# One pool of eight PSUM banks for attention, handed out by a run of the instruction list while building, with a new table of nominal times

## The chip, the cores and the metric

The kernel runs on one core of a Trainium2 chip. The metric is the device time of one execution in microseconds (us), taken as the median of several runs. The core's engines, as the profile names them, are PE (TensorE: matrix products, and PEld, its weight loads), ACT (ScalarE), DVE (VectorE), POOL (GpSimd) and SP (SyncE, which issues most transfers). Products land in PSUM, which has eight banks that hold 512 float32 numbers per partition each; ACT and DVE carry results from there to SBUF.

## What is computed

An attention over 2 batches of 8 heads, whose queries are first averaged in pairs along the sequence, then two feed-forward blocks. All inputs and the output are float32.

```python
# attention: q, k, v of (2, 8, 1152, 64)
q_pool = q.reshape(B, H, S // 2, 2, D).mean(axis=3)
scores = scale * np.matmul(q_pool, k.transpose(0, 1, 3, 2))
scores = scores - np.max(scores, axis=-1, keepdims=True)
attn = np.exp(scores)
attn = attn / (np.sum(attn, axis=-1, keepdims=True) + 1e-09)
x = np.matmul(attn, v)                      # -> (1152, 512) tokens
# first block, 512 -> 2048 -> 512
h = x @ w_in
g = (a[0] + a[1]*h + a[2]*h**2 + a[3]*h**3) / (1 + abs(b[0])*abs(h) + abs(b[1])*h**2 + 1e-6)
x = g @ w_out
# second block, 512 -> 2048 -> 512
h = x @ w_in2
out = (np.maximum(h, 0) + np.log1p(np.exp(-np.abs(h)))) @ w_out2
```

## The kernel before

Each float32 operand of a product is split into a high and a low part (names in `h` and `l`: `ph` and `pl`, `xh` and `xl`, `gh` and `gl`), and a product is made of two or three products of the parts.

**Attention** works on eight pairs of heads, j = 0 to 7. A pair has 1152 query rows in nine tiles of 128, numbered 9j to 9j+8, and each row tile has 1152 keys in three pieces of 384. For each row tile t and piece e there is:

- `score` (kind S, line 459): PE multiplies queries and keys into a tile `s` in PSUM
- `rmax` (M and B, lines 466 and 470): DVE takes the negated maximum `nm` of each piece, then `mb` of the three
- `expo` (E, line 479): ACT makes `p`, the exponentials, and their sums
- `spread` (T, line 430): PE transposes `p` in three pieces into a tile `t` in PSUM. In mode A, two tiles of three, ACT casts `t` to `ph` (V, line 425) and DVE subtracts for `pl` (L, line 313). In mode B, one of three, ACT copies `t` to `c` in SBUF (line 529), and POOL makes `ph` (H, line 539) and `pl` (L, line 313) of it
- `pv` (P, line 559): for four groups of row tiles per pair, PE sums 18 value products each into a tile `pv` in PSUM
- `norm` and `xev`: POOL and DVE make the reciprocals `rc` of the sums; PE transposes them (R, line 430) into PSUM; ACT copies one half of `pv` to `u` (U, line 589), DVE adds the other half (U1, line 592) and multiplies by the reciprocals into `xs` (U2, line 601); POOL splits `xs` into `xh` and `xl`.

During a pair the next one is prepared: transfers `kq`, sums `pq`, transpositions `kt` and `qt`, their splits, and transfers that lay the parts where the scores want them (`dk`, `dq`, `dd`). In the last pair thirteen blocks of weights are loaded and split for the feed-forward blocks (names `wraw`, `pk`, `w`; kinds wl, w0 to w4).

**Order.** Nothing is issued where it is written. `op` records each step with a nominal time `when`: its row tile's number plus an offset of its kind from the tables `O`, `OT` (by row tile) and `OJ` (first and last pair). `run` sorts each engine's steps by `when`; that is the order on the engine. Steps are then emitted, of those at the heads of the engines' lists whose needs are met the one with the lowest `when`.

**Banks.** PSUM is divided by purpose: `pS` has four banks for `s`, `pT` three for `t` (transpositions of probabilities, reciprocals, keys and queries alike), `pA` one for `pv`. Within each the tiles take turns in the order of `when` of their first step: the m-th `s` waits until all steps on the (m-4)-th `s` are done (`need[u[0]].update(tiles[m - n])`).

**After attention** the three pools are released and two pools for the first feed-forward block are made: `ph_`, two buffers of two banks each, in which PE multiplies tokens and weights into `h` (line 970), and `pa_`, four banks for the second product (line 1019). Each `h` is two blocks of 12 matmuls. ACT works on it at lines 986 to 988 (`act1_a`), DVE at 993 to 995 (`act1_y`), then both finish the activation. These steps are ordered by the framework's own scheduler, which may put them between attention's last ones. The second feed-forward block follows (lines 1051 and 1073).

## Time and profile before

| | us |
|---|---|
| median of 3 runs | 725.07 (724.95 to 726.0) |
| the profiled execution | 724.6 |
| its span, first to last instruction | 722.7 |
| attention, up to the last value product | 310.0 |
| from there to the end | 412.7 |

The profile has one execution. A page gives each engine's busy time and its course over 40 slices; other views give single instructions in order of time, what an engine waited for, and the chain of work that ended last. The rows that matter stand further down. A wait's releaser is the instruction whose end let the waiting one go, as far as the semaphores tell; `PEld s L459 <- ACT p L479` reads: the weight load of a score waited for an exponential.

### The profile page before, as it was taken

The page shows a single profiled execution, that of the slowest core. Times are in us where ns is not written, and L with a number is a line of the kernel's source. Part 1 is how long each engine was busy: PE and PEld are TensorE (multiplying, and loading weights), DVE is VectorE, ACT ScalarE, POOL GpSimd, SP SyncE. Part 2 cuts the span into 40 slices and gives each one's busy share as a digit, 9 for nine tenths or more (in the row PEclk, how much of TensorE's full clock was granted, in tenths as well). Part 3 has the DMA queues.
Part 4 walks back from the last instruction along what each step waited for, and adds up shares of the span by engine and source line. Part 5 has one row for each costly group of instructions (what it writes and reads, how often), then busy time and mean ns, then how long its engine had stood idle before and what let it go on. Part 6 is the DMA issues. An engine that isn't in the chain of part 4 may idle for free.

```text
span 722.7 us, 11854 instructions
## 1 busy us (share of the span) xinstructions
PE 685.3 (95%) x4076; PEld 629.0 (87%) x4076; DVE 559.4 (77%) x1080; ACT 495.2 (69%) x1135; POOL 205.2 (28%) x357
## 2 busy tenths in 40 slices
PE   7898999999999987879999999999999999999997
PEld 6788888888889876679999999999899998998996
DVE  4787889898988899989999999999776675612122
ACT  3788889999988889966777777776554464423221
POOL 3667686868685744630000000000000000000000
PEclk8999999999999999999999999999999999999999
DMA  3364647372727353431111112211034333201011
GB/s 98 100 132 115 151 116 158 95 185 62 165 54 165 91 159 130 148 115 59 59 58 59 59 59 88 88 29 59 2 117 126 107 117 99 77 1 45 0 44 44
DMA packets 60395, 65.68 MB, mean 91 GB/s; under 512 B 21552, under 2 KB 49456, under 8 KB 60336
## 3 DMA queue, kind: packets, MB, share of 16 engines
q1 hardware_dynamic: 59152, 63.95, 32.8%
q10 hardware_dynamic: 1184, 0.98, 0.4%
q8 instruction: 32, 0.52, 0.3%
q14 instruction: 27, 0.22, 0.1%
HBM read 47.71 MB, written 2.36 MB: 69 GB/s over the span
## 4 chain that ended last, share of the span: by engine, by line
PE 60%; DVE 19%; ACT 12%; issue 4%; DMA 2%; SPq 1%; POOL 0%; DVEq 0%; ACTq 0%
PE acc L1073 14%; PE h L1051 13%; PE s L459 8%; PE t L430 8%; PE pv L559 7%; PE acc L1019 5%; PE h L970 4%; ACT p L479 4%; DVE nm L466 2%; ACT ph L425 2%; DMA wraw<-in_moe_w_in_dram 2%; DVE m L995 2%; DVE p L993 2%; DVE m L1005 2%; DVE pl L313 2%
## 5 line engine op out<-in xcount | busy, mean ns | idle before, releaser
L466 DVE TENSOR_REDUCE nm<-s 128x1 f32<-128x384 f32 x216 | 116.5, 550 | 23.4 <-PE s L459 22.1
L479 ACT ACTIVATE p<-s,mb 128x384 f32<-128x384 f32 x216 | 125.9, 593 | 5.1 <-DVE mb L470 4.6
L313 DVE TENSOR_TENSOR gl<-p,gh 128x384 fp32r<-128x384 f32 (+1 forms) x72 | 49.6, 689 | 91.5 <-ACT gh L1060 89.7
L430 PE MATMUL t<-ident,p 128*128 128x128 f32 x648 | 99.0, 276 | 8.8 <-ACT p L479 4.2
L970 PE MATMUL h<-xh,w 128*128 128x384 f32 x384 | 98.5, 335 | 3.5 <-DVE p L994 3.5
L1051 PE MATMUL h<-xh,w 128*128 128x384 f32 x384 | 98.4, 336 | 0.0
L1059 ACT ACTIVATE p<-h 128x384 f32<-128x384 f32 x48 | 23.6, 492 | 108.5 <-PE h L1051 108.5
L1019 PE MATMUL acc<-gh,w 128*128 128x384 f32 x384 | 93.1, 337 | 2.1 <-ACT gh L980 2.1
L430 PEld LDWEIGHTS t<-ident,p 128*128 128x128 f32 x648 | 79.0, 142 | 18.2 <-ACT p L479 9.6
L559 PE MATMUL pv<-ph,v 128*128 128x256 f32 (+1 forms) x288 | 89.5, 321 | 1.2 <-DVE u L592 0.6
L1073 PE MATMUL acc<-w,gh 128*128 128x512 f32 x288 | 89.5, 392 | 0.0
L313 DVE TENSOR_TENSOR pl<-t,ph 128x384 fp32r<-128x384 f32 (+1 forms) x160 | 80.3, 509 | 7.0 <-ACT ph L425 5.4
L425 ACT CAST ph<-t 128x384 fp32r<-128x384 f32 (+1 forms) x160 | 70.0, 453 | 18.8 <-PE t L430 12.7
L559 PE MATMUL pv<-pl,v 128*64 128x256 f32 (+1 forms) x288 | 77.4, 295 | 1.6 <-POOL pl L313 1.6
L313 POOL TENSOR_TENSOR pl<-c,ph 128x384 fp32r<-128x384 f32 (+1 forms) x80 | 75.0, 941 | 4.6
L1051 PEld LDWEIGHTS h<-xh,w 128*128 128x128 f32 x384 | 70.5, 188 | 4.3 <-ACT p L1059 0.4
L970 PEld LDWEIGHTS h<-xh,w 128*128 128x128 f32 x384 | 69.1, 188 | 4.4 <-issue 4.3
L1019 PEld LDWEIGHTS acc<-gh,w 128*128 128x128 f32 x384 | 68.4, 188 | 4.5 <-ACT gh L980 4.5
L1051 PE MATMUL h<-xl,w 128*128 128x384 f32 x192 | 64.7, 337 | 0.0
L970 PE MATMUL h<-xl,w 128*128 128x384 f32 x192 | 64.3, 335 | 0.0
L539 POOL CAST ph<-c 128x384 fp32r<-128x384 f32 (+1 forms) x80 | 41.3, 520 | 71.6 <-ACT c L529 66.8
L1073 PEld LDWEIGHTS acc<-w,gh 128*128 128x128 f32 x288 | 53.4, 188 | 9.0
(129 smaller groups left out, 1493.5 us busy)
## 6 DMA issues: line engine op xcount, KB each, us to landing
wraw<-in_moe_w_in_dram SPq DMA_DIRECT2D x32, 512.0 KB, 3.8
wraw<-in_moe_w_out_dram SPq DMA_DIRECT2D x32, 512.0 KB, 3.3
vr<-in_v_dram SPq DMA_DIRECT2D x8, 576.0 KB, 5.0
kr<-in_k_dram SPq DMA_DIRECT2D x15, 288.0 KB, 5.4
qr<-in_q_dram SPq DMA_DIRECT2D x15, 256.0 KB, 5.1
out_dram<-m SPq DMA_DIRECT2D x15, 128.0 KB, 1.8
qq1a<-qhi SPq DMA_DIRECT2D x8, 144.0 KB, 2.5
ks1a<-khi SPq DMA_DIRECT2D x4, 288.0 KB, 3.2
```

The source lines that it names most:

```text
L313: return eng.tensor_tensor(out=o, in0=a, in1=b, op=ALU.subtract)
L425: nc.scalar.copy(out=out, in_=in_)
L430: nc.tensor.transpose(o[0:rows, i * 128:i * 128 + n], a, ident[0:n, 0:n])
L459: nc.tensor.matmul(out=o, lhsT=p, rhs=r, start=(m == 0), stop=(m == len(l) - 1))
L466: op("M" + str(n % 3), "DVE", fn=lambda: nc.vector.tensor_reduce(out=NM[i][:, n:n + 1], in_=tl[k], axis=AX.X, op=ALU.max, negate=True), R= ...
L479: nc.scalar.activation(out=o, in_=tl[k], func=AF.Exp, bias=MB[i][:, t:t + 1], accum_out=DEN[i][:, n:n + 1])
L539: nc.gpsimd.tensor_copy(out=view(h, o, w), in_=src(c, s0, w))
L559: nc.tensor.matmul(out=o, lhsT=p, rhs=r[:, m, 0:w], start=(c == a == 0), stop=(c == C - 1 and a == 1))
L970: nc.tensor.matmul(out=h, lhsT=w[:, wi, wd], rhs=x[:, d, xcols(c)], start=(n == 0), stop=(n == 3 * ND - 1))
L1019: nc.tensor.matmul(out=st["acc", c, d], lhsT=w[:, wi, wd], rhs=g, start=(first and n == 0), stop=(last and n == 2))
L1051: nc.tensor.matmul(out=h, lhsT=w[:, wi, d * 128:(d + 1) * 128], rhs=x[:, d, xcols(c)], start=(n == 0), stop=(n == len(mm) - 1))
L1073: nc.tensor.matmul(out=st["acc", c, t], lhsT=g[:, t * 128:(t + 1) * 128], rhs=w[:, wi], start=(first and n == 0), stop=(last and n == 2))
```

## The change

There are four parts.

1. The pools `pS`, `pT` and `pA` become one, `pB`, of eight banks. Every step that opens a PSUM tile (`score`, `spread`, `pair_k`, `pair_q`, `first_k`, `first_q`, `pv`, `xev`, `warm`) takes its tile from the ring `bk`.
2. `run` no longer emits by `when` alone. It runs the list with assumed durations and latencies: a step starts when its engine is free and its needs have ended. A step that opens a tile gets, of the banks whose tile has no step left to start, the one that comes free first by these durations. The steps are emitted in the order of these starts. The order on each engine is still that of `when`.
3. The assumed durations are changed a little (`act`, `dve`, `pool`, `mm`). They have no other use than in that run.
4. The tables `O`, `OT` and `OJ` have new numbers, so the order on each engine changes all over attention. Kinds get split names (W and Y for the copies of the other modes, N for POOL's low part). A table `OU` is added, with zeros alone, and `MODES` becomes a tuple with the same pattern for each pair.

The number of steps on each engine is the same.

```diff
-    "S0": -1.2121,
+    "S0": -1.113,
...
-MODES = "ABA"
-NS, NT_, NP_, NPH, NCP = 4, 3, 6, 5, 2
+MODES = ("ABA",) * 8
+NB, NP_, NPH, NCP = 8, 6, 5, 2
...
-        for n, tiles in rings.values():
+        after = [()] * len(ops)
+        opens, uses, left, free = {}, {}, {}, {}
+        for tag, (n, tiles) in rings.items():
+            if tag == "bk":
+                for k, u in enumerate(tiles):
+                    opens[u[0]], left[k], free[k] = k, len(u), 0
+                    for i in u:
+                        uses.setdefault(i, []).append(k)
+                continue
             tiles = sorted(tiles, key=lambda u: (ops[u[0]][0], u[0]))
             for m, u in enumerate(tiles):
                 if m:
-                    need[u[0]].add(tiles[m - 1][0])
+                    after[u[0]] += (tiles[m - 1][0],)
                 if m >= n:
                     need[u[0]].update(tiles[m - n])
...
-        done = [False] * len(ops)
+        start, lock, owner = {}, {}, [None] * NB
+        until = dict.fromkeys(queue, 0)
+
+        def ready(i):
+            e = ops[i][1]
+            a, bank = until[e], None
+            for d in need[i]:
+                if d not in start:
+                    return None
+                a = max(a, start[d] + ops[d][6] + (0 if e == ops[d][1] == "PE" else ops[d][7]))
...
+            if i in opens:
+                f = [(0 if k is None else free[k], b) for b, k in enumerate(owner) if k is None or not left[k]]
+                if not f:
+                    return None
+                a, bank = max(a, min(f)[0]), min(f)[1]
+            return max(a, lock.get(e, 0)) if ops[i][8] else a, i, bank
+
         with tc.manual_schedule():
             while any(queue.values()):
-                heads = [q[0] for q in queue.values() if q and all(done[d] for d in need[q[0]])]
-                i = min(heads, key=lambda i: (ops[i][0], i))
-                queue[ops[i][1]].pop(0)
-                done[i] = True
-                ops[i][2]()
+                a, i, bank = min(x for x in (ready(q[0]) for q in queue.values() if q) if x)
+                _, e, fn, _, _, _, ns, lat, port = ops[i]
+                queue[e].pop(0)
+                start[i], until[e] = a, a + ns
+                if bank is not None:
+                    owner[bank], st["bank", ("bk", opens[i])] = opens[i], bank
+                for k in uses.get(i, ()):
+                    left[k] -= 1
+                    free[k] = max(free[k], a + ns + (0 if e == "PE" else lat))
+                if port:
+                    lock["POOL" if e == "DVE" else "DVE"] = a + ns
+                fn()
...
-    pS = sb(name="pS", bufs=4, space=PSUM)
-    pT = sb(name="pT", bufs=3, space=PSUM)
-    pA = sb(name="pA", bufs=1, space=PSUM)
+    pB = sb(name="pB", bufs=1, space=PSUM)
...
     def act(n, extra=0):
-        return dict(ns=n * 0.917 + 50 + extra, lat=150)
+        return dict(ns=n * 0.833 + 45 + extra, lat=165)
...
+    def bank(k, name):
+        return pB.tile([128, 512], F32, tag="b" + str(st["bank", k]), name=name)
+
     def transpose(k, srcs, rows=128, w=128):
-        o = tl[k] = pT.tile([128, 512], F32, tag="t", name="t")
+        o = tl[k] = bank(k, "t")
...
-            o = tl[k] = pS.tile([128, 512], F32, tag="s", name="s")[:, 0:384]
+            o = tl[k] = bank(k, "s")[:, 0:384]
...
-        op("S" + str(e), "PE", fn=fn, R=R, W=[k], new=[("s", NS)], **mm(173 * (3 if diag else 2 * len(srcs))))
+        op("S" + str(e), "PE", fn=fn, R=R, W=[k], new=[("bk", NB)], **mm(173 * (3 if diag else 2 * len(srcs))))
```

What this moves is shown at three places. In these lists a row is one instruction, with the line and, in brackets, the engines or transfers whose semaphores it waits for; line numbers of the changed kernel are 84 higher or so (514 for 430, 543 for 459, 643 for 559, 613 for 529, 673 for 589).

PE in the middle of pair 3, around the transposition of reciprocals (`rc`) of its second group; `ks1b`, `qq1b` and `ql1b` are keys and queries of the pair's second head. Before:

```order
L459 MATMUL s<-ks1b,qq1b 128x384 [waits DMAHW5_49,DMAHW7_49,DMAHW4_49,DMAHW0_49]
L459 MATMUL s<-ks1b,ql1b 128x384 [waits DMAHW1_49]
L430 MATMUL t<-ident,rc_67 64x128 [waits Activation_49]
L430 MATMUL t<-ident,rc_67 64x128
L459 MATMUL s<-ks1b,qq1b 128x384 [waits Activation_49]
L459 MATMUL s<-ks1b,ql1b 128x384
L430 MATMUL t<-ident,p 128x128 [waits DVE_49]
L430 MATMUL t<-ident,p 128x128 x2
L459 MATMUL s<-ks1b,qq1b 128x384 [waits Activation_49]
L459 MATMUL s<-ks1b,ql1b 128x384
```

After:

```order
L514 MATMUL t<-ident,rc_67 64x128 x2
L543 MATMUL s<-ks1b,qq1b 128x384 [waits DMAHW2_49,DMAHW1_49,DVE_49]
L543 MATMUL s<-ks1b,ql1b 128x384
L543 MATMUL s<-ks1b,qq1b 128x384 [waits DVE_49]
L543 MATMUL s<-ks1b,ql1b 128x384
L543 MATMUL s<-ks1b,qq1b 128x384 [waits Activation_49]
L543 MATMUL s<-ks1b,ql1b 128x384
L543 MATMUL s<-ks1b,qq1b 128x384 [waits DVE_49]
L543 MATMUL s<-ks1b,ql1b 128x384
L514 MATMUL t<-ident,p 128x128 [waits Activation_49]
L514 MATMUL t<-ident,p 128x128 x2
```

The transposition of reciprocals has moved ahead of the first of these scores and shows no wait of its own; four scores stand in a row behind it, on banks that transposed tiles and a value tile held.

ACT in the last row tile of attention, where the last copy `c` is made (`w` and `pk` are weight preparation). Before:

```order
L425 CAST ph<-t 128x3x128 [waits PE_49]
L479 ACTIVATE p,den_63<-s,mb_65 128x384 [waits Activation_49]
L365 ACTIVATE pk<-wraw 128x512 [waits DMAHW0_49,DVE_49,Activation_49]
L425 CAST ph<-t 128x3x128 [waits PE_49]
L870 CAST w<-pk 128x512 [waits DVE_49]
L589 COPY u<-pv 64x320 [waits PE_49]
L529 COPY c<-t 128x384 [waits PE_49,Pool_49]
```

After:

```order
L563 ACTIVATE p,den_63<-s,mb_65 128x384
L506 CAST ph<-t 128x3x128 [waits PE_49]
L446 ACTIVATE pk<-wraw 128x512 [waits DMAHW0_49,DVE_49]
L613 COPY c<-t 128x384 [waits PE_49,Pool_49]
L673 COPY u<-pv 64x320 [waits PE_49]
L954 CAST w<-pk 128x512 [waits DVE_49]
L506 CAST ph<-t 128x3x128 [waits PE_49]
```

The last exponential has moved ahead of a cast, and the copy `c` ahead of a cast `ph`, a weight cast and the copy `u`.

PE where attention ends (`h` is the first feed-forward product). Before:

```order
L430 MATMUL t<-ident,p 128x128 x2
L430 MATMUL t<-ident,rc_67 64x128 [waits DVE_49]
L970 MATMUL h<-xh,w 128x384 x2
L970 MATMUL h<-xl,w 128x384
L970 MATMUL h<-xh,w 128x384 x2
L970 MATMUL h<-xl,w 128x384
L970 MATMUL h<-xh,w 128x384 x2
L430 MATMUL t<-ident,rc_67 64x128 [waits DVE_49]
L430 MATMUL t<-ident,rc_67 64x128
L970 MATMUL h<-xl,w 128x384
L559 MATMUL pv<-ph,v_115 128x256 [waits DVE_49]
```

After:

```order
L643 MATMUL pv<-ph,v_109 128x256 [waits Activation_49]
L643 MATMUL pv<-pl,v_109 64x256 [waits DVE_49]
L643 MATMUL pv<-ph,v_109 128x256
L643 MATMUL pv<-pl,v_109 64x256 x2
L643 MATMUL pv<-ph,v_109 128x256
L514 MATMUL t<-ident,rc_67 64x128 [waits DVE_49]
L514 MATMUL t<-ident,rc_67 64x128
L1054 MATMUL h<-xh,w 128x384 [waits DVE_49,Activation_49]
L1054 MATMUL h<-xh,w 128x384
```

Before, nine matmuls of `h` stand ahead of the last group's value products; now the first one stands behind all of attention and waits for DVE and ACT. Its two banks are the lowest of the pool, and there the last value tile and the last tile of reciprocals lie.

## Rows read from the trace of the kernel before

**Rows 1.** The page, part 1: busy us, share of the span and instructions.

```profile
PE 685.3 (95%) x4076; PEld 629.0 (87%) x4076; DVE 559.4 (77%) x1080; ACT 495.2 (69%) x1135; POOL 205.2 (28%) x357
```

**Rows 2.** Windows: length, busy us (instructions) of each engine, granted clock, DMA share, GB/s.

```profile
12.60:19.40 6.80, 5.99 (x24) 5.31 (x24) 3.97 (x10) 4.59 (x13) 1.67 (x3) 0.50 0.00 0
...
36.00:254.00 218.00, 208.38 (x1467) 187.79 (x1468) 189.23 (x469) 194.11 (x586) 154.89 (x274) 1.00 0.54 124
254.00:310.00 56.00, 45.19 (x296) 37.94 (x296) 53.99 (x124) 49.67 (x134) 29.28 (x46) 1.00 0.48 146
...
361.00:722.70 361.70, 355.80 (x1889) 334.35 (x1889) 246.31 (x365) 194.37 (x309) 0.00 (x0) 1.00 0.21 64
```

**Rows 3.** Waits of weight loads, 36 to 254: us in total, times, longest.

```profile
PEld s L459 <- ACT p L479: 10.7, 18, 0.8
PEld t L430 <- ACT c L529: 6.8, 20, 0.6
PEld t L430 <- ACT p L479: 2.9, 7, 1.3
...
PEld pv L559 <- DVE u L592: 1.0, 3, 0.3
```

**Rows 4.** Chain that ended last, by time: start, us, what.

```profile
15.06 1.92 PE t L430 x9
...
126.06 0.98 PE t L430 x9
160.62 0.98 PE t L430 x9
...
389.94 4.16 PE h L970 x24
```

**Rows 5.** Timeline of PE in pair 3: start, us, instruction [idle before, releaser].

```profile
138.75 0.41 PE L430 MATMUL t<-ident,rc 128*64 128x128 f32 x2
139.72 0.45 PE L459 MATMUL s<-ks1b,qq1b 128*128 128x384 f32 x1 [0.56 <-ACT p L479]
...
143.55 0.44 PE L459 MATMUL s<-ks1b,qq1b 128*128 128x384 f32 x1 [0.30 <-ACT p L479]
...
158.98 0.28 PE L559 MATMUL pv<-pl,v 128*64 128x256 f32 x1
159.40 0.44 PE L459 MATMUL s<-ks0a,qq0a 128*128 128x384 f32 x1
```

**Rows 6.** Timeline of PE at the start.

```profile
13.41 0.69 PE L459 MATMUL s<-ks0a,qq0a 128*128 128x384 f32 x1 [1.42 <-ACT p L479]
```

**Rows 7.** Waits of weight loads, 254 to 311.

```profile
PEld t L430 <- ACT p L479: 6.7, 7, 1.9
PEld s L459 <- ACT p L479: 3.7, 6, 1.0
```

**Rows 8.** Timeline of PE where attention ends.

```profile
304.54 0.60 PE L970 MATMUL h<-xh,w 128*128 128x384 f32 x2
...
310.01 0.34 PE L970 MATMUL h<-xh,w 128*128 128x384 f32 x1
```

**Rows 9.** Timeline of ACT there.

```profile
304.13 0.49 ACT L425 CAST ph<-t 128x384 fp32r<-128x384 f32 x1
...
305.61 0.48 ACT L529 COPY c<-t 128x384 f32<-128x384 f32 x1
...
313.03 0.99 ACT L986 ACTIVATE p<-h,a_sb 128x768 f32<-128x768 f32 x1 [0.59 <-PE h L970]
...
318.48 0.68 ACT L365 ACTIVATE pk<-wraw 128x512 f32<-128x512 f32 x1 [1.60 <-DMA wraw<-in_moe_w_in_dram]
319.06 0.98 ACT L986 ACTIVATE p<-h,a_sb 128x768 f32<-128x768 f32 x1
```

**Rows 10.** Timeline of DVE there.

```profile
312.48 0.42 DVE L601 TENSOR_TENSOR xs<-t,u 64x256 f32<-64x256 f32 x1
...
321.56 0.96 DVE L993 TENSOR_TENSOR p<-h,p 128x768 f32<-128x768 f32 x1 [1.33 <-ACT s L988]
```

More of the change, by code (lines that the diff above doesn't have):

```diff
@@ new lines @@
+    "S2": -0.7975,
+    "M0": -0.8979,
+    "M1": -0.941,
+    "M2": -0.5959,
+    "B": -0.298,
+    "E0": -0.1842,
+    "E1": -0.2218,
+    "E2": -0.1057,
+    "T0": -0.0926,
+    "T1": -0.02,
+    "T2": 0.3759,
+    "V0": 0.3479,
+    "V1": 0.4004,
+    "V2": 0.2985,
+    "H0": 0.4679,
+    "H1": 0.057,
+    "H2": 0.4185,
+    "L0": 0.8887,
+    "L1": 0.7005,
+    "L2": 0.8988,
+    "D0": 0.9909,
+    "D1": 1.9757,
+    "R": 2.6459,
+    "U": 2.3672,
+    "U1": 2.601,
+    "U2": 2.8694,
+    "X0": 4.1997,
@@ new lines @@
+    "w0": -0.694,
+    "w1": -0.353,
+    "w2": 0.1327,
+    "w3": 0.2942,
+    "w4": 0.8642,
+    "wl": -2.9198,
+    "W0": 0.3479,
+    "Y0": 0.3479,
+    "N0": 0.5179,
+    "W1": 0.4004,
+    "Y1": 0.4004,
+    "N1": 0.7005,
+    "W2": 0.2985,
+    "Y2": 0.2985,
+    "N2": 0.4685,
+    "vw0": 5.5844,
+    "vw1": 4.225,
+    "fh": -0.6739,
+    "fp": 3.618,
+    "fl": 0.9103,
+    "fa": -0.6404,
+    "P0": 1.1291,
+    "P1": 0.5424,
+    "P2": 0.5433,
+    "P3": 1.2299,
+    "P4": 1.4149,
+    "P5": 2.1976,
@@ L554, in fn @@
                 if c == 0:
-                    tl[k] = pA.tile([128, 512], F32, tag="a", name="pv")
+                    tl[k] = bank(k, "pv")
                 acc, v2 = tl[k][:, 0:w], V2[i][:, x]
```

321 lines of the change are left out of this document (141 added, 180 removed), and 105 rows, old and new, of tables (OT, OU).

## The prediction

> **What bounds the kernel now.** I read the page first, then the stretches, then the waits inside them. PE is busy for 95% of the span [rows 1], and its granted clock reads 1.00, that is 2.4 GHz, in every stretch from 36 us on [rows 2]: the kernel is a TensorE kernel, and time can only come from PE standing still or being slow. The stretches [rows 2] show where. From 361 us to the end PE works 355.80 of 361.70 us; the change doesn't touch that part. In the middle pairs of attention, 36 to 254 us, PE is busy 208.38 of 218.00 us, but ScalarE has 194.11 and VectorE 189.23, so three engines are nearly full and feed each other through PSUM. In the last pair, 254 to 310 us, PE falls to 45.19 of 56.00 and VectorE has 53.99: there the weight preparation sets the pace.
>
> The busy time of PE hides part of its standing still, because each run of matmuls counts its own drain. The waits of the weight loads show it better [rows 3]: 10.7 us before scores, ended by an exponential; 6.8 us before transpositions, ended by the plain copy `c`; 2.9 us before transpositions, ended by an exponential (that is data: the probabilities themselves); 1.0 us before the value products, ended by the evacuation `u`. The first, second and fourth are banks: the queries and keys of a score lie ready for long, and only the bank is missing. The pattern repeats with the pair: the same nine transpositions begin at 126.06 and at 160.62 us, so a pair takes 34.56 us [rows 4]. In one pair the reciprocal transposition at 138.75 us is followed by a score only at 139.72 us, with 0.56 us of plain idleness after the exponential, the score at 143.55 us has idled 0.30 us for another exponential, and the one at 159.40 us starts 0.42 us behind a value product whose own step is about 0.12 us, so 0.30 us late [rows 5].
>
> **The change, part by part.** The work is the same: as many instructions of each kind, the same matmuls. Three things move: which bank an opening instruction takes, the order on each engine (the tables), and what stands where attention ends.
>
> *Middle pairs (36 to 254 us, 218.00/34.56 = 6.3 pairs).* Before, every score waits for the exponential four scores back. A score's chain to that point is a reduction, a minimum and an exponential, so a score that stands just behind has to idle. In the new order the four scores behind the reciprocal transposition stand in a row, and all four open banks that held transposed or value tiles, none of them a score's that still waits for its exponential (the first pair of lists in the section on the change). Of the score waits the place behind the reciprocals and the one behind the second value product should vanish and the one behind the key transposition should stay; in the pair looked at that is 0.56 + 0.30 gone of 0.56 + 0.30 + 0.30, or 74%. I take a little less, 7.4 of the 10.7 us. Of three reciprocal transpositions per pair that wait for a copy, two now open banks freed by an exponential more than 4 us of PE work back, and the third stays close behind a copy: half, 3.4 us. The 1.0 us before value products goes, since they no longer share a single bank. Together 11.8 us.
>
> Against that stand new short distances. Counting PE's own work in the new order (4.16/24 = 0.173 us a matmul of 384 columns, 0.98/9 = 0.109 us a transposition [rows 4]), six openings of a pair follow the transposition whose copy must free their bank by only 0.8 to 1.0 us. The nearest row for such an opening is the reciprocal transposition at 138.75 us, which waited for a copy and lost about 0.13 us [rows 5]. 6 x 0.13 x 6.3 = 4.9 us. The cover is ScalarE being on time; if it is late by one exponential, this is the slower rival below. Net: 4.9 - 11.8 = **-6.9 us**. The bounds: at best all bank waits go and none comes, 10.7 + 6.8 + 1.0 = 18.5 us gained; at worst nothing goes and the six cost their 4.9 us.
>
> *Start.* At 13.41 us the first score of the second tile has idled 1.42 us for an exponential, and nine transpositions at 15.06 us follow at half the granted clock, 0.50 or 1.2 GHz from 12.6 to 19.4 us [rows 2, 4, 6]. With eight banks open two scores of that tile run before, in the idle time, and the transpositions come next. At most 15.06 - 13.41 = 1.65 us; I take **-1.0**, since one score of that tile still stands among the transpositions. Should the filled gap keep the clock up, the same nine transpositions would take 0.98 instead of 1.92 us; over 6.8 us that is at most 3.4 us more, kept for the range.
>
> *Last pair.* The waits before transpositions (6.7 us) and scores (3.7 us) [rows 7] end with exponentials, but those are late because of the weights: VectorE has 2.0 us left in 56.00 [rows 2]. So the pool buys nothing I would count there; bounds 0 and 2.0 us. One move is certain: the last plain copy `c`, which starts the last chain over GpSimd, stood at 305.61 us behind a cast, a weight cast and a `u` [rows 9]; now it comes ahead of all three (second pair of lists). It can start where the cast at 304.13 us stood: 305.61 - 304.13 = 1.48 us earlier, and with it the last value products. I take **-1.4**.
>
> *Where attention ends.* Before, the first product of the MoE (L970) opened banks of the score pool, free early: nine of its matmuls ran from 304.54 us, ahead of the last value products, and the rest followed at 310.01 us without a wait [rows 8]. The new pool's first two banks belong at the end to the last value product and the last reciprocal tile (third pair of lists): the first matmul now waits for ScalarE's `u` and VectorE's last two steps. Counted from the last value product: the `u` and two products of about 0.4 us each with one weight step between, some 2.0 us (before they ended at 312.48 + 0.42, with two weight steps between [rows 10]). Then 24 matmuls are 4.16 us per pair of blocks [rows 4]: the first activation starts at +6.3 us instead of +3.0 (313.03 [rows 9]), the second at +10.4 instead of +9.05 (319.06). The chain runs through the second, where ScalarE waited 1.60 us for a weight transfer and VectorE 1.33 us for ScalarE [rows 9, 10]. So +1.4, less a little that VectorE does of the weights meanwhile: **+1.2**. Bounds: 0, if the weights are late anyway, and 4.2 us, the whole first block.
>
> The SyncE order moves too (the query and key transfers of the next pair change places, the next loads come earlier), but scores stand some ten microseconds behind them, nothing on PE waits for a transfer in [rows 3], and I cost it at 0.
>
> *Sum.* -6.9 - 1.0 - 1.4 + 1.2 = -8.1 us. The profiled execution took 724.6 us (span 722.7 and 1.9 around it), 0.5 us below the median of the runs; 724.6 - 8.1 = **716.5 us**.
>
> **A rule weighed.** PE's granted clock is 1.00 in the windows from 36 us on although PE stopped for banks all along there [rows 2, 3]; only the stretch at the start shows 0.50. The Trainium skill, "TensorE: Matmul & The Clock Gate", section "A second HAM failure mode: psum-queue depth-cycling", says that cycling through PSUM banks with small idle times between groups of matmuls can make the clock oscillate, which speaks against one ring over eight banks. By that rule the time would be longer; the trace of before, which cycles through eight banks already, doesn't agree. As a mechanism of this kernel, one further stretch like that at the start would cost up to 3.4 us (half of 6.8 us); since idle times should get shorter, I give it 2 in 100, as part of the slower case.
>
> **The rivals.** *Larger gain.* The new tables put every opening behind a bank that is really free. For it: the order shows waits on long-finished work at most openings. Against: ScalarE at 89% and VectorE at 87% leave little room for queues. 18.5 + 1.0 + 1.4 - 1.2 = 19.7 us gained: 704.9 us; half-way between it and the forecast begins its ground, about 711. *No change.* ScalarE sets the pace of the pairs, and PE's waits only change their name, from banks to probabilities: the middle gives 0, and -1.0 - 1.4 + 1.2 is lost or not with VectorE's load of the last pair: 723.4 to 726. For it: 194.11 of 218 us. Against: 11% of idle time, part of it waits for PE's transpositions. *Slower.* A bank is fixed while building. At the six close openings of each pair PE, which works in order, must wait for that one bank even if another is free. If ScalarE runs one exponential behind (the score that waits 0.56 us in [rows 5] shows the size), each loses 0.56 instead of 0.13 us: 6 x 0.56 x 6.3 = 21.2 us against 11.8 gained, so 724.6 + 9.4 - 1.0 - 1.4 + 1.2 = 732.8 us. It decides from about 11.8/(6 x 6.3) = 0.31 us per opening. That the pool doesn't do what it says I leave out: the lists show other engines in the waits.
>
> **How the numbers follow.** Forecast (711 to 721 us): 0.57. Larger gain: 0.18. No change: 0.11. Slower: 0.14, the clock's 0.02 in it. What a measurement can tell from no change is 0.2%, 1.45 us. Faster: 0.57 + 0.18 = 0.75 and a little of the no-change case, 0.77; same 0.10; slower 0.13. The range runs from 706.5, which leaves about 0.09 of the larger gain out, to 725.5, which leaves about 0.11 of the slower case out.
>
> **What would show it.** Right: the pair's period falls from 34.56 us to about 33.4, the weight loads' waits for exponentials before scores to about a third, and the first L970 product starts behind the last `xs` with an idle PE of about 2 us. Wrong: the waits stay near 25 us under new names (plain copies, `gl` parts, `xs`), the clock falls below 1.00 after 36 us, or the gap at the end of attention reaches 4 us. The last 361.7 us should not change.

## The result and the profile after

The changed kernel took 714.33 us (711.51 to 714.97, 4 runs) beside 725.01 us (724.63 to 726.0) for the kernel before on the same chip: a ratio of 0.984, 95% interval 0.981 to 0.987. That is 10.7 us less, where 8.1 were predicted. The profiled execution is the shortest of the four, 711.51 us with a span of 709.4. Run again on another chip (e12 below) the kernel took 714.08 us (712.56 to 714.26) beside 726.10, 0.983 [0.981, 0.985]; its profiled execution took 712.56 us, its span 710.5. Where the two traces differ, both are given.

Windows of the changed kernel answer [rows 2] (window, length, busy us of PE, PEld, DVE, ACT and POOL with the number of instructions, granted clock, DMA share, GB/s). The second window is the middle of attention, cut where the same work now lies.

```profile
12.60:19.40 6.80, 5.75 (x40) 4.66 (x40) 6.29 (x16) 6.80 (x22) 3.40 (x8) 1.00 0.13 39
31.00:240.00 209.00, 205.88 (x1471) 191.28 (x1471) 186.57 (x473) 192.76 (x585) 155.97 (x272) 0.99 0.57 128
```

In the middle PE now stands still, by its busy time, for 3.1 us of 209, where it was 9.6 of 218 [rows 2]. The waits of its weight loads in the same window (us in total, times, longest) answer [rows 3]:

```profile
PEld pv L643 <- DVE pl L396: 3.3, 10, 0.7
PEld t L514 <- ACT p L563: 3.2, 13, 0.3
PEld t L514 <- DVE qlo L816: 1.9, 1, 1.9
PEld s L543 <- DVE klo L396: 0.9, 3, 0.3
...
PEld s L543 <- DVE u L676: 0.5, 3, 0.2
```

The 10.7 us before scores and the 6.8 us before transpositions that ended with a `c` are gone altogether. What is left is mostly data: value parts, probabilities. The 1.9 us for `qlo` go back to a transfer (e4 below). Only the last two lines shown are banks, 1.4 us.

To see where the time went, take one instruction as a mark, the transposition of the last reciprocals of a pair (two matmuls, so "x2"; the rows at 33.66 and 26.88 us, and those that end the four pairs below, are that of a pair's first reciprocals). Its rows in the timeline of PE (start, us, instruction, and in brackets the idle time ahead of it and what ended it), first before:

```profile
33.66 0.38 PE L430 MATMUL t<-ident,rc 128*64 128x128 f32 x2
...
62.44 0.41 PE L430 MATMUL t<-ident,rc 128*64 128x128 f32 x2 [0.27 <-ACT c L529]
96.59 0.41 PE L430 MATMUL t<-ident,rc 128*64 128x128 f32 x2
...
242.18 0.41 PE L430 MATMUL t<-ident,rc 128*64 128x128 f32 x2
...
310.18 0.38 PE L430 MATMUL t<-ident,rc 128*64 128x128 f32 x2
```

The changed kernel:

```profile
26.88 0.38 PE L514 MATMUL t<-ident,rc 128*64 128x128 f32 x2
...
53.11 0.38 PE L514 MATMUL t<-ident,rc 128*64 128x128 f32 x2
88.81 0.38 PE L514 MATMUL t<-ident,rc 128*64 128x128 f32 x2
...
121.91 0.38 PE L514 MATMUL t<-ident,rc 128*64 128x128 f32 x2
...
227.97 0.38 PE L514 MATMUL t<-ident,rc 128*64 128x128 f32 x2
...
296.88 0.41 PE L514 MATMUL t<-ident,rc 128*64 128x128 f32 x2 [0.51 <-DVE rc L660]
```

The changed kernel again:

```profile
54.89 0.38 PE L514 MATMUL t<-ident,rc 128*64 128x128 f32 x2
...
89.20 0.38 PE L514 MATMUL t<-ident,rc 128*64 128x128 f32 x2
...
228.97 0.38 PE L514 MATMUL t<-ident,rc 128*64 128x128 f32 x2
...
297.18 0.41 PE L514 MATMUL t<-ident,rc 128*64 128x128 f32 x2 [0.46 <-DVE rc L660]
```

| stretch, by the marks of before | before | after | again |
|---|---|---|---|
| start and pair 0, up to 62.44 | 62.44 | 53.11 (-9.3) | 54.89 (-7.6) |
| pair 1, to 96.59 | 34.15 | 35.70 (+1.6) | 34.31 (+0.2) |
| "four pairs", 96.59 to 242.18 | 145.59 | 139.16 (-6.4) | 139.77 (-5.8) |
| rest of attention, to 310.18 | 68.00 | 68.91 (+0.9) | 68.21 (+0.2) |
| behind attention, to the span's end | 412.5 | 412.5 (0.0) | 413.3 (+0.8) |

(The "four pairs" run from the last mark of pair 1 to the first mark of pair 6, so they are a little more than four; the two marks are the same instructions in every kernel, so this stretch serves as the measure below.) A pair takes 121.91 - 88.81 = 33.10 us, where it took 34.56 [rows 4]. Over half of the gain lies ahead of the middle pairs, and pair 1 gives some back. Part of the first line, and of the loss in the fourth, is only the mark's place: in the new order it stands about 0.8 us earlier (of the nine transpositions from 91.33 us before, the last six are the ones at 84.69 us after; three steps of 0.11 us into their row they began at 91.66 us, so they moved by 7.0 us, where the mark beside them moved by 7.8). So the rest of attention took about as long as before.

### The profile page after: what moved, and what is told of

Read it like the earlier page. It is cut to its first block, busy times and chain, and to the rows that moved or that the text cites. A ratio compares the mean times of both kernels' runs of the same rounds, so it can differ in the third digit from the quotient of the medians.

```text
span 709.4 us, 11830 instructions
## 1 busy us (share of the span) xinstructions
PE 681.0 (96%) x4076; PEld 633.2 (89%) x4076; DVE 556.5 (78%) x1080; ACT 493.5 (70%) x1135; POOL 207.3 (29%) x357
## 4 chain that ended last, share of the span: by engine, by line
PE 62%; DVE 15%; ACT 13%; DMA 4%; issue 4%; SPq 1%; ACTq 0%; DVEq 0%
PE acc L1157 14%; PE h L1135 14%; PE t L514 8%; PE pv L643 8%; PE s L543 8%; PE acc L1103 5%; PE h L1054 5%; ACT p L563 4%; DMA wraw<-in_moe_w_in_dram 3%; DVE p L1077 2%; DVE m L1089 2%; DVE m L1079 2%; ACT ph L506 2%; DVE p L1088 1%; ACT c L613 1%
## 5 line engine op out<-in xcount | busy, mean ns | idle before, releaser
L550 DVE TENSOR_REDUCE nm<-s 128x1 f32<-128x384 f32 x216 | 111.7, 550 | 12.6 <-PE s L543 11.1
L514 PE MATMUL t<-ident,p 128*128 128x128 f32 x648 | 102.0, 277 | 8.4 <-ACT p L563 6.1
L1054 PE MATMUL h<-xh,w 128*128 128x384 f32 x384 | 99.4, 338 | 3.5 <-DVE p L1078 2.5
L396 DVE TENSOR_TENSOR pl<-t,ph 128x384 fp32r<-128x384 f32 (+1 forms) x160 | 78.6, 510 | 4.4 <-ACT ph L506 3.7
L1054 PEld LDWEIGHTS h<-xh,w 128*128 128x128 f32 x384 | 70.1, 190 | 4.4 <-issue 4.3
L1054 PE MATMUL h<-xl,w 128*128 128x384 f32 x192 | 64.8, 338 | 0.0
L1103 PE MATMUL acc<-gl,w 128*128 128x384 f32 x192 | 59.1, 335 | 0.0
```

Of the source, the lines that this page charges most:

```text
L396: return eng.tensor_tensor(out=o, in0=a, in1=b, op=ALU.subtract)
L514: nc.tensor.transpose(o[0:rows, i * 128:i * 128 + n], a, ident[0:n, 0:n])
L550: op("M" + str(n % 3), "DVE", fn=lambda: nc.vector.tensor_reduce(out=NM[i][:, n:n + 1], in_=tl[k], axis=AX.X, op=ALU.max, negate=True), R= ...
L1054: nc.tensor.matmul(out=h, lhsT=w[:, wi, wd], rhs=x[:, d, xcols(c)], start=(n == 0), stop=(n == 3 * ND - 1))
L1103: nc.tensor.matmul(out=st["acc", c, d], lhsT=w[:, wi, wd], rhs=g, start=(first and n == 0), stop=(last and n == 2))
```

## The experiments

Three questions: is it the pool or the new tables that shortens a pair (theory A: a free bank is nearly always at hand, against the order by itself); what holds pair 1 up; and why the rest of attention gained nothing.

### The pool alone (e1)

The tables of before on the new pool.

```diff
 O = {
-    "S0": -1.113, "S1": -1.3915, ...
+    "S0": -1.2121, "S1": -1.3786, ...
```

> The tables of before (order on every engine as before) on one pool of eight banks handed out by the run while building. Theory A (free banks make the gain, any order can use them): a middle pair falls from 34.56 us by at least 1.0 us of the 1.5 us that the change gave, and the kernel is near 718 us. Theory B (the gain is the new order, which the pool only makes possible): the waits for exponentials before scores lose their bank part, but the scores stand where they stood, a pair stays within 0.4 us of 34.56 and the kernel within 722 to 726 us. Where attention ends, the first product of the feed-forward block opens the two lowest banks in both.

713.96 us (713.03 to 716.06) beside 725.72, 0.984 [0.983, 0.986]. Its marks, and the largest wait of a weight load from 33 to 243 us:

```profile
59.33 0.41 PE L474 MATMUL t<-ident,rc 128*64 128x128 f32 x2 [0.37 <-ACT c L573]
...
91.94 0.41 PE L474 MATMUL t<-ident,rc 128*64 128x128 f32 x2
...
232.41 0.41 PE L474 MATMUL t<-ident,rc 128*64 128x128 f32 x2
```

```profile
PEld t L474 <- ACT c L573: 6.6, 18, 0.7
```

The four pairs take 140.47 us: the pool alone brings 5.1 of the 6.4 us. The score waits vanish even in the old order; the transpositions still wait for a `c`, as long as before (6.8 us [rows 3]). That wait is what the new order takes away. They also wait 6.2 us for an exponential, where it was 2.9 [rows 3]: part of the time that PE lost for banks it now loses for data.

In all, the pool alone is as fast as the changed kernel: both ratios are 0.984, and the time is 4 us under what theory A expected. By e1's marks (59.33, 91.94, 232.41 and 299.24 us, span 712.3) the start and pair 0 take 59.33 us, pair 1 32.61, the four pairs 140.47, the rest of attention 66.83, and 413.1 lie behind. So the new tables gain 6.2 us ahead of pair 1 (first trace; 4.4 in the second) and 1.3 us in the four pairs (0.7), and lose 3.1 us in pair 1 (1.7) and 2.1 us in the rest of attention (1.4). What remains, 2.9 and 1.8 us of span, does not show in the medians.

### The new tables without the pool (e2b, e5)

e2b runs the new tables for pairs 0 to 6 (and the old ones in the last pair) on the three old pools; e5 runs the same tables on the pool of eight. One offset had to be moved in both so that three pools can run that order at all.

```diff
-    "kl0": (-0.3135, 0),
+    "kl0": (-0.58, 0),
...
+        o, ot, oj = (B_O, B_OT, B_OJ) if j >= 7 else (O, OT, OJ)
```

> The new tables in pairs 0 to 6 on the three pools of before (four, three and one bank), the last pair and its weights by the old tables; one split of the first pair (kl0) stands a little earlier so that the order can be run at all. Theory A (free banks): scores that stand four in a row wait for exponentials again, a pair takes 35 us or more, the kernel is slower than 725 us. Theory B (order): a pair stays at about 33.1 to 33.6 us and the kernel at 714 to 718 us. Middle: 34 us a pair, both halves count.

> The same mixture of tables as in e2b (pairs 0 to 6 by the changed kernel's numbers, the last pair by the old kernel's, kl0 at -0.58), but on the pool of eight. If it is the split into three pools that these numbers cannot bear (theory A), a middle pair takes 33.0 to 33.3 us as in the changed kernel, against 38.1 us in e2b, and the time is 712 to 717 us. If it is the mixture itself (the joint between the tables, or the kl0 step) that made e2b slow, this is slow too: over 35 us a pair and over 730 us.

e2b: 746.3 us (745.1 to 750.2), 1.029 [1.026, 1.033]. e5: 713.33 us (711.9 to 714.25) beside 725.01, 0.983 [0.981, 0.986]. The marks of e2b, then those of e5, then e2b's largest wait from 36 to 275 us:

```profile
99.59 0.38 PE L673 MATMUL t<-ident,rc 128*64 128x128 f32 x2
...
260.12 0.41 PE L673 MATMUL t<-ident,rc 128*64 128x128 f32 x2
```

```profile
88.69 0.38 PE L709 MATMUL t<-ident,rc 128*64 128x128 f32 x2
...
228.30 0.38 PE L709 MATMUL t<-ident,rc 128*64 128x128 f32 x2
```

```profile
PEld s L702 <- ACT p L722: 26.2, 49, 0.9
```

The four pairs take 160.53 us on three pools and 139.61 us on one. The new order is no better order by itself: four scores in a row on four score banks wait for exponentials, 26.2 us of them. It is an order for a common pool, and is worth 1.3 us of four pairs there (139.16 against 140.47). That e5 takes 139.61 us also clears the moved offset and the joint between the tables: neither makes e2b slow.

### One bank less (e6)

```diff
-NB, NP_, NPH, NCP = 8, 6, 5, 2
+NB, NP_, NPH, NCP = 7, 6, 5, 2
```

> The changed kernel with seven banks in the pool instead of eight; the instruction order is the same, only the handing differs. In the nominal run of the changed kernel 30 of the 444 openings between 36 and 254 us take the last free bank, so with seven these have to wait. If the gain comes from an opening nearly always finding a bank that is free (theory A), those 30, at a few tenths each, cost 0.5 to 2 us a pair: 33.5 to 35 us a pair and 718 to 727 us in all, and waits for exponentials, copies and max reductions are back among the weight loads that transpositions and scores make. If it is the one common order of handing that counts and not the number of banks, seven do as well as eight: 713 to 716 us.

739.48 us (737.78 to 741.72), 1.020 [1.017, 1.023]. Marks, and waits from 36 to 264 us:

```profile
95.53 0.38 PE L514 MATMUL t<-ident,rc 128*64 128x128 f32 x2
...
248.81 0.41 PE L514 MATMUL t<-ident,rc 128*64 128x128 f32 x2
```

```profile
PEld pv L643 <- ACT c L613: 4.0, 9, 0.6
PEld t L514 <- ACT c L613: 3.5, 10, 0.4
...
PEld s L543 <- ACT p L563: 2.1, 6, 0.4
```

153.28 us for the four pairs, 14.1 more than with eight and even 7.7 more than three fixed pools of eight banks in their own order. Theory A holds, and the price was underrated: up to 2 us a pair and 727 us in all were expected, a pair takes 131.91 - 95.53 = 36.38 us, 3.3 more than 33.10, and the time is over 739 us. The waits come back at every kind of opening. That a late opening delays the evacuations which later ones need, and so multiplies the price, is a guess that no run here tests. The Trainium skill, "Perfetto Trace Analysis", section "Matmul Optimizations", says to use all eight banks; seven against eight agrees, while before and e1 both use all eight, and which tile may have which bank is worth 5.1 us of four pairs.

That the banks are handed out by a simulated run, and not simply in turn, wasn't tried on the chip: by the lists of steps such an order stops early in pair 0, in the old tables as in the new, since a transposition of row tile 1 needs a bank whose exponential stands on ACT behind a step that waits for that transposition.

### The durations of the simulated run (e11)

```diff
-        return dict(ns=n * 0.833 + 45 + extra, lat=165)
+        return dict(ns=n * 0.917 + 50 + extra, lat=150)
...
-        return dict(ns=n, lat=205)
+        return dict(ns=n, lat=240)
...
```

> The changed kernel with the old kernel's assumed durations and latencies (ScalarE 0.917 ns per column and 50 ns, against 0.833 and 45; PE's latency 240 against 205 ns and so on) in the simulated run; the order on every engine is the same, only the handing of banks can differ. If the handing is fed well enough by any durations that are about right, the period of a pair stays within 0.2 us of 32.8 us and the time within 1.5 us of the changed kernel's. If it needs the new ones, openings get banks that come free late, and the time is over 718 us.

711.84 us (711.52 to 712.45) beside 726.10, 0.981 [0.979, 0.982], where the changed kernel on the same chip had 0.983 [0.981, 0.985]. Its four pairs take 227.56 - 88.59 = 138.97 us, as with the new durations (139.16 and 139.77). By the lists, only 24 of the 542 openings follow another tile on their bank than in the changed kernel. The handing doesn't need the new durations; whether the old ones are better by the 2.2 us between the medians stays open, since the intervals touch.

### What holds pair 1 up (e4)

```diff
-    "dd": (1.5635, 0),
+    "dd": (-2.25, 0),
```

This moves the loads of pair 1 that lay `qhi` and `qlo` into `qdh` and `qdl` (kind dd) ahead of the loads of `qq1b` and `ks1b` in SyncE's order, nothing else.

> The changed kernel with four transfers of the first preparation (dd, from qhi and qlo) four places earlier in SyncE's queue, ahead of the second query transfers. In the changed kernel ScalarE waits 1.92 us for them at 54.00 us, PE idles until 55.14 us, and its clock reads 0.50 from 56.9 to 60.3 us. Theory C (the idle time costs itself and a slow stretch behind it): both vanish, 3 to 3.5 us faster than the changed kernel in runs that had both, about 711 us. Rival (the next thing is as late: the sums or the transposition behind the same queue): under 1 us, and the slow stretch stays.

710.44 us (709.03 to 712.16) beside 725.72, 0.980 [0.978, 0.982]. ScalarE's row for pair 1's `qhi`, which is written over what these loads still read: before, in the changed kernel, in e4.

```profile
60.07 0.49 ACT L727 ACTIVATE qhi<-t 128x384 fp32r<-128x384 f32 x1 [1.64 <-DMA qdl<-qlo]
```

```profile
54.00 0.49 ACT L811 ACTIVATE qhi<-t 128x384 fp32r<-128x384 f32 x1 [1.92 <-DMA qdh<-qhi]
```

```profile
51.84 0.50 ACT L811 ACTIVATE qhi<-t 128x384 fp32r<-128x384 f32 x1
```

SyncE's row for the load, in the changed kernel and in e4; PE's row that waits for it, and the window behind it, in the changed kernel:

```profile
48.82 2.49 SPq L517 DMA_DIRECT2D qdh<-qhi  x2
```

```profile
45.22 1.24 SPq L517 DMA_DIRECT2D qdh<-qhi  x2
```

```profile
55.14 0.55 PE L514 MATMUL t<-ident,p 128*128 128x128 f32 x3 [1.65 <-DVE qlo L816]
```

```profile
56.90:60.30 3.40, 3.40 (x15) 3.30 (x14) 1.90 (x6) 1.74 (x6) 1.50 (x3) 0.50 0.49 105
```

The stall was there before too (1.64 us on ScalarE). Attention now arrives earlier and the load comes after the same queue of other loads, so the stall takes back part of what the start gained, and in this trace PE's idle time was followed by 3.4 us at the half clock. Without both, pair 1 takes 85.05 - 52.98 = 32.07 us (e4's marks) instead of 35.70: 3.6 us. The second trace of the changed kernel has the stall without the slow stretch (e12 below) and takes 34.31 us there: 2.2 us are the stall's, the other 1.4 the clock's. e4's median is 3.9 us under the changed kernel's; the two intervals ([0.978, 0.982] and [0.981, 0.987]) just meet.

### The end of attention (e3, e7)

e3 makes the pool of the second product ahead of the pool of `h`, so that the first `h` lies on banks that come free early.

```diff
+        pa_ = sb(name="pa", bufs=4, space=PSUM)
         ph_ = sb(name="ph", bufs=2, space=PSUM)
-        pa_ = sb(name="pa", bufs=4, space=PSUM)
...
```

> The changed kernel with the two pools after attention made in the other order, so that the first feed-forward product opens banks 4 to 7, which are free early, and the second product's sums get banks 0 to 3. My term for the end of attention (+1.2 us, the first matmul at 298.15 us waits 0.86 us for the last xs and has no work ahead of the last value products): 1 to 2 us faster than the changed kernel, about 713 us. Rival (the weights are late anyway: ScalarE waits 1.89 us for a weight transfer just ahead of the first activation at 303.77 us): no difference over 0.4 us.

712.90 us (711.46 to 714.19) beside 725.72, 0.982 [0.981, 0.984]. That is 1.4 us under the changed kernel's median and near the 713 us expected, but the intervals overlap, so the time doesn't decide; the rows do. PE and ScalarE at that place in the changed kernel:

```profile
298.15 0.59 PE L1054 MATMUL h<-xh,w 128*128 128x384 f32 x2 [0.86 <-DVE xs L685]
...
309.24 0.78 PE L1054 MATMUL h<-xh,w 128*128 128x384 f32 x2 [2.52 <-DVE p L1078]
```

```profile
303.08 0.66 ACT L446 ACTIVATE pk<-wraw 128x512 f32<-128x512 f32 x1 [1.89 <-DMA wraw<-in_moe_w_in_dram]
303.77 0.99 ACT L1070 ACTIVATE p<-h,a_sb 128x768 f32<-128x768 f32 x1
```

And in e3:

```profile
308.77 0.98 PE L1054 MATMUL h<-xh,w 128*128 128x384 f32 x2 [3.92 <-DVE p L1078]
```

```profile
302.61 0.67 ACT L446 ACTIVATE pk<-wraw 128x512 f32<-128x512 f32 x1 [1.51 <-DMA wraw<-in_moe_w_in_dram]
303.30 0.99 ACT L1070 ACTIVATE p<-h,a_sb 128x768 f32<-128x768 f32 x1
```

The 0.86 us ahead of the first `h` product are gone, and the wait ahead of the third `h` has grown from 2.52 to 3.92 us. In both kernels the first activation stands on ScalarE right behind a weight step that waits for its transfer. From the last reciprocals to that activation it is 303.77 - 296.88 = 6.9 us in the changed kernel and 303.30 - 296.11 = 7.2 us in e3, and to the end of the span 412.5 us and 710.8 - 296.11 = 414.7 us. So the free bank gains nothing here: the transfer sets the time of the activation, and the bank only decides on which side of the `h` products PE idles.

e7 is e3's and e4's edits together.

> Two edits together: the three loads of QD moved ahead (as in e4, which took 710.4 us) and the first hidden tiles put on banks that come free early (as in e3). In e4's trace the first h matmul waits 1.54 us for the last xs and the first activation waits 0.80 us for h, so that the bank is on the path there; in e3 it was not, since the activation stood behind a weight step that waited for its DMA. If the bank wait counts where the activation waits for h, this gains up to 0.8 us on e4: 709.6 to 710.4 us, and the first h starts within 0.5 us of the last transposition's end. If the time behind attention is set by the weights' DMAs, it is the same as e4 within 0.3 us, and the time saved before the first h comes back as a longer wait for the first p.

711.37 us (710.75 to 712.80) beside 725.01, 0.981 [0.978, 0.984], no gain on e4. The activation that waited for `h` in e4 again stands behind a late weight step, and PE's wait for `p` is 3.89 us, where it was 1.35 in e4: the second of the two expectations.

### The last pair (e9, e10)

e9 does the two steps of DVE that put the bits of a weight together on half the columns (of the weights made during attention); it leaves the other half out.

```diff
+    def w_half(i, n):
+        raw, g = st["raw", i], st["pk", i][:, :256]
...
-        op("w1", "DVE", fn=lambda: w_conv(i, 0), R=[pk], W=[pk], port=True, ns=340, lat=150)
...
+        op("w1", "DVE", fn=lambda: w_half(i, 0), R=[pk], W=[pk], port=True, ns=340, lat=150)
...
```

> The changed kernel, with the two DVE steps that put the weights' bits together in place (the shift and the merge, 0.60 and 0.74 us each, 6 of each between 270 and 297 us) done on 256 of the 512 columns for the weights that are made during attention; this leaves out half of those weights' conversion. It takes some 0.3 us off each, 3 to 4 us of DVE's 25.4 busy of 26.7 us from 270.2 to 296.9. If DVE is what bounds the last pair in both kernels (theory D: why no bank wait that was removed there made it shorter), the stretch from the last pair's fifth slot to its last pv product gets 2 to 3.5 us shorter, about 711 to 712.5 us in all. If PE's chain through ACT bounds it, it gets shorter by less than 0.7 us, and the time is 713.5 to 715 us.

e10 is e4 with every second low half of these weights made on GpSimd, and leaves nothing out.

```diff
-            sub(nc.vector, w[:, 1], g, w[:, 0])
+            sub(nc.gpsimd if i % 2 else nc.vector, w[:, 1], g, w[:, 0])
...
```

> e4 with the low half of every second weight that is made during attention subtracted by GpSimd instead of DVE. In the last pair 3 or 4 such steps of 0.79 us leave DVE, which is busy 24.7 of 26.6 us there, and go to GpSimd, which is busy 15.1. If DVE's own work bounds the last pair (theory D) the stretch from the last pair's fifth slot to its last transposition gets 1.5 to 2.5 us shorter, and the time is 708 to 709.5 us. If GpSimd's work slows DVE's, or the weights come too late for the first h products, nothing is gained: 710 to 713 us.

e9 took 708.49 us (707.63 to 710.56) beside 725.01, 0.977 [0.975, 0.980]; e10 710.10 us (708.89 to 712.38) beside 726.10, 0.978 [0.976, 0.980]. The same piece of the last pair, from its fifth slot to its last reciprocals, in windows of before, the changed kernel, its second trace, e9, e4 and e10 (length, then busy PE, PEld, DVE, ACT, POOL, and the clock):

```profile
284.60:310.20 25.60, 20.05 (x133) 16.73 (x132) 24.59 (x56) 21.84 (x59) 15.30 (x24) 1.00 0.45 145
```

```profile
270.20:296.90 26.70, 19.86 (x121) 16.14 (x119) 25.42 (x55) 22.68 (x60) 15.28 (x23) 0.94 0.41 136
```

```profile
271.64:297.18 25.54, 19.13 (x119) 16.01 (x119) 24.75 (x55) 22.46 (x59) 13.76 (x23) 0.94 0.44 140
```

```profile
270.90:295.30 24.40, 18.33 (x121) 14.70 (x120) 23.20 (x55) 22.48 (x60) 13.89 (x23) 1.00 0.46 151
```

```profile
266.60:293.20 26.60, 19.89 (x120) 16.15 (x118) 24.68 (x54) 22.65 (x60) 15.13 (x23) 0.94 0.42 134
```

```profile
269.80:294.30 24.50, 19.41 (x120) 16.16 (x119) 22.62 (x51) 22.11 (x59) 18.65 (x26) 0.93 0.43 140
```

DVE is busy 25.4 of 26.7 us and 24.75 of 25.54. Taking 2.2 us of its work out made the stretch 2.3 us shorter than in the first trace (e9), and handing 2.1 us of it to GpSimd made it 2.1 us shorter than in e4 (e10). Against the second trace both gain only 1.1 and 1.0 us, and the clock is not the same in all: e9's piece ran at 1.00, the others but the one of before have some 3 us at the half clock in them. So DVE's work is on the path of the last pair, at 1.0 to 2.3 us for some 2 us of it, and a free bank has little to give there; that nothing else is on it isn't shown.

The times don't fit the expectations as well as the pieces do. e9 is 2.5 us below the lower end of its range, and this piece explains less than half of its 5.8 us. e10 lies at the lower end of the range for no gain and is not told apart from e4 (0.978 [0.976, 0.980] and 0.980 [0.978, 0.982], on different chips). Its profiled execution is 2.3 us later than e4's at the last mark of pair 0 (55.24 and 52.98 us): as in e12 below, its start ran at the half clock, which takes back in the trace what the last pair gained.

### The changed kernel again (e12), and the edits together (e13)

> The changed kernel once more, without an edit. Its first profile fell on the shortest of its runs (711.5 us, the others 714.1 to 715.0) and showed no stretch at half the granted clock in the first 50 us; the trials with the same start showed one of 6.8 us there, and their T0 of pair 0's fifth slot came 1.0 to 2.1 us later. If that stretch makes the difference between the runs, a run at 714 us shows it and is later by 1 to 2 us at 30 us. If the wait for the load of qdh at 53 to 55 us takes up what the start loses, the ninth slots' times from 84 us on are the same as in the first profile within 0.5 us, and the 2.5 us between the runs must come from another place, behind attention.

The row of e12's start, against 12.6 to 19.4 us of the changed kernel's first trace above:

```profile
11.70:18.50 6.80, 5.93 (x24) 5.07 (x23) 4.75 (x13) 4.72 (x15) 2.68 (x6) 0.50 0.00 0
```

The same program ran that stretch at the half clock here and at the full clock there. That costs 1.8 us at the first mark of the table (54.89 against 53.11) and 0.4 us at the second (89.20 against 88.81). The wait for `qdh` does not take up the difference, as the expectation supposed it might: the load itself comes 1.8 us later (50.62 against 48.82 us), and behind the wait this trace is still 2.0 us late (57.14 against 55.14). PE's row behind the wait here, and the middle of attention here and in e4:

```profile
57.14 0.55 PE L514 MATMUL t<-ident,p 128*128 128x128 f32 x3 [1.87 <-DVE qlo L816]
```

```profile
31.00:240.00 209.00, 204.91 (x1474) 189.54 (x1472) 187.24 (x476) 193.29 (x590) 156.68 (x273) 1.00 0.56 128
```

```profile
36.00:240.00 204.00, 202.92 (x1464) 189.15 (x1462) 183.50 (x462) 189.99 (x578) 154.06 (x267) 1.00 0.59 136
```

The first trace ran at the half clock from 56.9 to 60.3 us; this one kept 1.00, though PE had idled longer. There the first trace loses 1.6 us of its lead: it is 0.4 us ahead when pair 1's first reciprocals are transposed (64.55 against 64.97 us). Further on the second trace is 1.0 us late (228.97 against 227.97 us), so the times stay the same within 0.5 us for a part of attention only.

So the start's clock may well be part of the 2.5 us between the shortest run and the others, which no trace shows, since the profiled executions were the shortest. The single runs have a mean granted clock of 0.992 and 0.993 in these two executions and of 0.985 to 0.990 in the six longer ones (714.05 to 714.97 us), so those ran more of their time at the half clock. That this is the whole difference isn't shown: e11's shortest run, 711.52 us, has 0.986.

e13 is e4, e10 and e11 in one.

> The three edits that gained, together: the loads of QD moved ahead (e4), the low half of every second weight on GpSimd (e10), and the old durations in the simulated run (e11). e10 took 710.1 us and e11 711.8 where the changed kernel took 714.1 us on the same chip. If the durations' gain is one of its own, 708 to 709 us; if it was the same gain (both end the wait of 3.5 us in the first pair, or both shorten the last), 709.5 to 711 us, no less than e10.

710.15 us (708.74 to 710.81) beside 725.65, 0.978 [0.977, 0.980]: the second expectation, no better than e10. In its trace the piece of the last pair is as short as in e10, but from the last marks of pair 5 on (216.37 to 255.27 us, 38.9 us; in e4 216.63 to 253.14, 36.5 us) it had lost 2.4 us in pair 6, in part at the half clock (251.9 to 255.3 us reads 0.53). The gains do not add up here, and why isn't shown.

## Why the prediction was near, and where its terms were off

The forecast was 716.5 us, the time is 714.33. The mechanism of the middle pairs was named rightly: with a common pool the waits for banks go (e1, e6). That the sum came within 2.2 us is in part luck: the start was priced at a fraction of what it gave, which made up for a loss that was not seen (pair 1) and a gain that did not come (the last pair).

- **Middle pairs, -6.9: right in kind, too small.** A pair was to take about 33.4 us and takes 33.10. Over the 6.3 pairs that makes (34.56 - 33.10) x 6.3 = 9.2 us, pair 1's loss not counted. The pool alone gives most of it (5.1 of 6.4 us of four pairs, e1). The term that failed is the price of the six close openings, 4.9 us at 0.13 us each: no wait for a `c` is left in the middle. It takes pool and order together: such waits are 6.6 us in e1, with the old order on eight banks, and 3.7 us in e2b, with the new order on three pools. The removed waits were also more than the 11.8 us counted (17 us by the two lists of waits). That not all of it shows has one visible reason: value products now wait 3.3 us for `pl`, a wait that the list of before doesn't have. That copies would still be waited for was wrong; that other waits would take some of the gain was right.
- **Start, -1.0: the step that failed.** The stretch up to 36 us was looked at for one wait and one stretch of low clock, and the gain by banks was counted from 36 us on, with 1.1 us a pair. But pair 0 runs on the same banks from its first tile. Its first mark, at 33.66 us before, comes at 26.88 us in the first trace and at 28.69 in the second: 6.8 and 5.0 us were gained where 1.0 was counted, some 0.7 us of it by the mark's place (two scores that stood ahead of it now stand behind). Start and pair 0 together gained 7.6 us with the low clock at the start and 9.3 us without it. The pool alone gives 62.44 - 59.33 = 3.1 us (e1's mark there is at 59.33 us, and its start ran at 1.00 too, so part of this is the clock); the new tables give the other 6.2 us of the first trace: from 10 to 36 us the weight loads waited 7.7 us before, 4.6 of them for exponentials ahead of scores, and in the changed kernel they wait 3.8 us up to 31 us, none ahead of a score for an exponential. The one wait that was priced, 1.42 us at 13.41 us, was not the longest of its kind: a score at 33.21 us waited 1.69 us. The part kept for the range, the clock, is 1.8 us of the 3.4 allowed, and it varies between executions of one program.
- **SyncE's order, 0: wrong.** "Nothing on PE waits for a transfer" overlooked that a transfer can be waited for because it *reads*: ScalarE may not write the next `qhi` before the load has taken the last one. The changed kernel loses 3.6 us there in the first trace and 2.2 in the second, against e4.
- **Last pair, -1.4: wrong.** The copy `c` moved ahead in ScalarE's order, but not in time: it starts 4.6 us ahead of the last mark before (305.61 and 310.18 us) and after (292.29 and 296.88 us). The prediction's own row says that DVE had 2.0 us left in 56.00, and e9 and e10 show that DVE's work is on the path. The piece of the last pair in the windows above takes 26.70 us, where it took 25.60, with 3.4 us at the half clock in it; in the second trace it takes 297.18 - 271.64 = 25.54 us, with 2.9 us at the half clock.
- **End of attention, +1.2: its lower bound, 0.** The first L1054 product does start behind the last `xs`, after 0.86 us of idle time (1.55 in the second trace) instead of 2. But the weights are late anyway, which was the reason given for the bound (e3). Behind the last reciprocals it takes 412.5 and 413.3 us, before 412.5.
- **Rivals.** The larger gain came true in kind (bank waits nearly all gone) and not in size: of the 18.5 us that it counts on, 9.2 came, and what PE no longer loses for banks it loses in part for data, for the load of `qdh` and for DVE. No change, with ScalarE as the pace of the pairs, is ruled out by the shorter pairs, but its remark that waits would change their name holds for part of them (e1's 6.2 us). The slower rival, one late bank stopping PE, is not in the changed kernel but is what e6 and e2b are: both orders with one bank too few where it is needed.
- **The rule weighed.** PE's clock did fall below 1.00 in the middle of the first trace, at one place, behind the 1.65 us of idle time in pair 1. In the second trace, which is the same program and idles 1.87 us there, and in e4, which doesn't idle there, the middle has 1.00. All three cycle through the same eight banks, so the cycling alone doesn't make the clock oscillate here; the idle time alone doesn't lower it either, and what does stays open.

## What to carry to other kernels

When scarce buffers are split by purpose, price the split by what stands queued for one part while another is free; the pool alone gave the whole measured gain here. An order made for the pool gave another fifth in the middle pairs, lost elsewhere what it won, and is worse than the old one without the pool. Read the utilization of the stretch ahead of the waits in it: where another engine is busy for 95%, removing PE's waits for banks may gain nothing. And look at who reads a buffer last, transfers too, before writing off a queue as harmless.

## What was not expected of the hardware

The granted clock of the same program differed from run to run in the same stretch (1.00 and 0.50 in the first 20 us, 1.8 us apart). In the first trace of the changed kernel three stretches at 0.50, of 3.4 us each, came behind idle times of PE of 1.65, 1.89 and 2.52 us. In the second trace the same three waits lasted 1.87, 1.89 and 2.62 us, and the clock stayed at 1.00 behind each; its one later stretch at 0.50, from 271.2 to 274.6 us, came behind idle times of 0.93 us and less. So the length of one idle time doesn't tell here whether the clock falls. The 2.2 us by which the old durations came out ahead are unexplained.
